# Block-sparse attention with a gated two-layer block behind it, one core: another load order at the start, weights and layer two moved, output stores on another queue

## The chip, the cores and the metric

The kernel runs on one core of one Trainium2 chip. The metric is the device time of one execution in microseconds, the median of several. A core has five engines that each work through their own list of instructions in order: PE (TensorE), DVE (VectorE), ACT (ScalarE), POOL (GpSimd) and SP (SyncE, which here only issues DMAs and loads registers). ACT and POOL issue DMAs too. They wait for each other through semaphores.

## The reference

Inputs are q, k, v of shape 4 x 8 x 768 x 64 (batches, heads, rows, width), three sampled block numbers for each of 24 blocks of 32 rows, and the weights of the second layer: w_in 512 x 1024, w_out 1024 x 512, g_ln 1024. `window` is 1. The heads of layer one's result are put side by side to x, 3072 x 512.

```python
    scores = scale * np.matmul(q, k.transpose(0, 1, 3, 2))
...
    mask = np.abs(blk_i - blk_j) <= window
    mask = mask | (blk_i == 0) | (blk_j == 0) | (blk_i == n_blocks - 1) | (blk_j == n_blocks - 1)
    for qb in range(n_blocks):
        for kb in sampled_blocks[qb]:
            mask[qb * block:(qb + 1) * block, kb * block:(kb + 1) * block] = True
    scores = np.where(mask, scores, -1000000000.0)
...
    attn = np.exp(scores)
    attn = attn / (np.sum(attn, axis=-1, keepdims=True) + 1e-09)
    return np.matmul(attn, v).astype(np.float32)
...
    h = x @ w_in
    h_max = np.max(h, axis=-1, keepdims=True)
    e = np.exp(h - h_max)
    sm = e / (np.sum(e, axis=-1, keepdims=True) + 1e-09)
    solu = h * sm
    mu = np.mean(solu, axis=-1, keepdims=True)
    var = np.mean((solu - mu) ** 2, axis=-1, keepdims=True)
    ln = (solu - mu) / np.sqrt(var + 1e-06) * g_ln
    return (ln @ w_out).astype(np.float32)
```

## The kernel before

**Layer one.** The work of a batch is four pairs of heads (16 pairs in all). k and q come from DRAM as float32, two heads to a DMA of 384 KB (`load_kq`, L302), are cast to bf16 (`cast_kq`, L310) and turned by PE (`turn_kq`, L316) into `kT` and `qT`. v comes in six DMAs of 256 KB (`load_v`, L325), is cast into `vbuf` (`cast_v`, L331), and the whole of it is written back to DRAM as bf16 rows (`save_v`, L335), so that the sampled blocks can be gathered from there. For each of 22 blocks of queries, `gather_k` (L364) copies the sampled key blocks inside SBUF, on POOL, DVE or ACT, and `gather_v` (L383) fetches the sampled value rows: as one indirect DMA on POOL, or as three or four plain DMAs on SP or ACT, whose addresses are loaded into registers first. `glob_k` and `glob_v` copy the first and the last block. `score_static` (L412) makes the scores of the band and of the first and last blocks in three parts, `score_rand` (L456) those of the sampled blocks in two. ACT takes exponentials into `pst` and `prd`, DVE multiplies by the band mask (L450). `out_list` and `out_mms` multiply by v in a first part that needs no gathered values and a second part that does (L507), and `normalise` writes `xb`.

**Layer two.** Tiles of 128 rows go in eight groups of three. `moe_x` (L534) turns `xb` into `xT` by three DMA transposes on SP; there is one `xT` buffer. A group is 15 steps: eight of `moe_f` (L547: four matmuls into the PSUM tile `hps`, an exponential on ACT, a product on DVE into `soluT`), one of `moe_s` (L562: sums), and six of `moe_o` (L598: two for each of three tiles; ACT scales the PSUM tile `ops` into `ot`, L610). `hps`, `ops` and the turned k and q share two PSUM buffers, `p_h`. `ot` has two buffers. The store of an `ot` tile is put off (`put_out`, L616): SP issues it just ahead of the next tile's `ot`, or at the next group's first step.

**Order.** The lists of the engines are in the order of the program, written out by hand. A loop over slots `s` (L780) deals out the work: six slots to a pair, layer one's parts first, then one step of layer two from slot `MOE0 = 31` on (two in every fourth slot, and two in each slot once layer one is done), then the loads, casts, turns and gathers. For batch `nb`, `f = s - 24 (nb - 1)` says when its loads, casts and gathers are issued (L835 to L860). The last slot of a batch's layer one is `s = 28, 52, 76, 100`; there `put_rows` and `moe_x` follow.

**Start.** Before the loop (L680 to L766) SP and ACT issue loads of k and q of batch 0, then v. All use the pool `raw`, which has four buffers, so that a load waits until an earlier one has been cast. DVE makes the tables of addresses (L704 to L743), then clears buffers (L744 to L760), then casts v. The remaining q of batch 0 is loaded in slots 0 to 2, and batch 0's gathers are dealt out in slots 3 to 5. In slot 5 POOL issues the load of `w_in` (L825, with a cast to bf16) and ACT those of `g_ln` and of `w_out` (`load_w`, L640: one DMA of 2 MB into `w_f`, which takes one of the two buffers of the pool `vgp`, tag `vg`, that the gathered values use). DVE scales `w_out` in slots 8 to 15 (`scale_w`) and takes its mean off it in slots 18 to 25 (`centre_w`).

Of the kernel before, what the change touches and what calls it, by code (L numbers as in the profile page):

```python
# [201 lines left out]
def kernel(  # L202
# [11 lines left out]
    nc = tc.nc  # L214
# [87 lines left out]
    def load_kq(b, which, a, eng):  # L302

        rw = raw.tile([TQ, 2, NT, D], FP32, tag="raw", name=f"raw{which}{b}_{a}")
        eng.dma_start(
            out=rw.rearrange("p h i d -> p h (i d)"),
            in_=(k, q)[which][b, 2 * a : 2 * a + 2].rearrange("h (p i) d -> p h (i d)", i=NT))
        staged[which, b, a] = rw
# [16 lines left out]
    def load_v(b, c, eng):  # L325
        rw = raw.tile([TQ, HD], FP32, tag="raw", name=f"rawv{b}_{c}")
        eng.dma_start(out=rw.rearrange("p (h d) -> p h d", h=H),
                      in_=v[b, :, c * TQ : (c + 1) * TQ, :].rearrange("h p d -> p h d"))
        staged[2, b, c] = rw
# [18 lines left out]
    def glob_k(b):  # L348
        z = kgz[b % 2]
        src = kTs[b].rearrange("p a (n o) -> p a n o", o=BLK)  # L350
        for par in range(2):
            lo = par * 64
            nc.gpsimd.tensor_copy(
                out=z[lo : lo + 64, :, lo : lo + 64].rearrange("p a (n o) -> p a n o", o=BLK),
                in_=src[lo : lo + 64, :, 0 : NB : NB - 1, :])
# [191 lines left out]
    def moe_f(g, f):  # L547
        hps = p_h.tile([128, GN], FP32, tag="h")
        for c in range(KD):
            nc.tensor.matmul(hps, w_in_sb[:, c, f * 128 : (f + 1) * 128], xTs[g][:, c, :],  # L550
                             start=(c == 0), stop=(c == KD - 1))
        if f == 0:
            sums_of[g] = p_sum.tile([128, 512], FP32, tag="sums", name=f"sums{g}")
        else:
            moe_e(g, f - 1)
        eTs[g, f] = mo3.tile([128, GN], BF16, tag="eT", name=f"eT{g}_{f}")
        nc.scalar.activation(out=eTs[g, f], in_=hps, func=ACT.Exp, scale=1.0)  # L557
        nc.vector.tensor_tensor(out=soluT[:, f, :, 0:128],  # L558
                                in0=hps.rearrange("p (i x) -> p i x", i=GT),
                                in1=eTs[g, f].rearrange("p (i x) -> p i x", i=GT), op=ALU.mult)  # L560
# [37 lines left out]
    def moe_o(g, i, half):  # L598
# [6 lines left out]
        if half == 1:  # L605
            if i == 0:
                moe_r(g)
            put_out()
            ot = mo.tile([128, d_model], FP32, tag="ot")
            nc.scalar.activation(out=ot, in_=o_ps.pop(t), func=ACT.Copy,  # L610
                                 scale=rstds[g][:, i : i + 1])
            ots.append((t, ot))

    ots = []

    def put_out():  # L616
        while ots:
            t, ot = ots.pop()
            nc.sync.dma_start(out=out[t * 128 : (t + 1) * 128, :], in_=ot)
# [3 lines left out]
    def moe_step(n):  # L623
# [3 lines left out]
        if r == 0:  # L627
            put_out()
# [10 lines left out]

    def load_w():  # L640
        w_f.append(vgp.tile([128, KF, d_model], FP32, tag="vg", name="w_f"))
        nc.scalar.dma_start(out=w_f[0], in_=moe_w_out.rearrange("(c p) m -> p c m", p=128))

    w_f = []

    def scale_w(c):
        nc.vector.tensor_scalar(out=w_out_sb[:, c, :], in0=w_f[0][:, c, :],
                                scalar1=g_ln_sb[:, c : c + 1], scalar2=None, op0=ALU.mult)
# [32 lines left out]
    load_kq(0, 0, 0, nc.sync)  # L681
    load_kq(0, 1, 0, nc.scalar)
    load_kq(0, 0, 1, nc.sync)
    load_kq(0, 0, 2, nc.scalar)
    cast_kq(0, 0, 0, nc.gpsimd.tensor_copy)
    cast_kq(0, 1, 0, nc.scalar.copy)
    load_kq(0, 0, 3, nc.sync)
    load_v(0, 0, nc.scalar)
    turn_kq(0, 0, 0, nc.scalar.copy)
    turn_kq(0, 1, 0, nc.scalar.copy)  # L690
    for c in range(3):
        cast_kq(0, 0, c + 1, nc.gpsimd.tensor_copy)
        load_v(0, c + 1, nc.sync)
# [50 lines left out]
    for vb in vbuf:  # L744
        nc.vector.memset(vb[:, :, :, D:D1], 1.0)
    zero_v = prd_p.tile([TQ, 2 * n_ed * BLK], BF16, tag="prd1", name="zero_v")
    nc.vector.memset(zero_v, 0.0)
    for b in range(B):
        nc.sync.dma_start(out=v_scr[b][NB * BLK :, :], in_=zero_v[0:BLK, 0 : H * D1])


    band = setup.tile([TQ, NCH, TQ], BF16, name="band")
    nc.vector.memset(band, 1.0)
    for j, i0, i1 in ((0, 2, 4), (1, 3, 4), (2, 0, 1), (3, 0, 2)):
        nc.vector.memset(band[j * BLK : (j + 1) * BLK, :, i0 * BLK : i1 * BLK], 0.0)
    nc.vector.memset(band[0:BLK, 0, :], 0.0)
    nc.vector.memset(band[TQ - BLK :, NCH - 1, :], 0.0)
    for z in kgz:
        nc.vector.memset(z, 0.0)
    nc.vector.memset(soluT[:, :, :, 128:D2], 1.0)  # L760
    for c in range(2):
        cast_v(0, c, nc.vector.tensor_copy)
        load_v(0, c + 4, nc.sync)
    for c in range(2, NCH):
        cast_v(0, c, (nc.vector.tensor_copy, nc.gpsimd.tensor_copy)[c % 2])
    save_v(0, 0, NCH, nc.sync)  # L766
    nc.vector.memset(mean_w, 1.0 / d_ff)
# [7 lines left out]
    MOE0 = 31  # L775
# [4 lines left out]
    while step < N_STEPS:  # L780
# [28 lines left out]
        if s < 3:  # L809
            load_kq(0, 1, s + 1, nc.sync)  # L810
        if 1 <= s < 4:
            turn_kq(0, 0, s, nc.scalar.copy)
        if s == 3:
            glob_k(0)
            glob_v(0, nc.gpsimd.tensor_copy)
        if 3 <= s < 6:
            cast_kq(0, 1, s - 2, nc.vector.tensor_copy)
            turn_kq(0, 1, s - 2, nc.vector.tensor_copy)
        if 3 <= s < 6:
            for i in range((s - 3) * 8, min((s - 2) * 8, n_gk)):  # L820
                gather_k(0, i, on=(1, 0, 1, 2)[i % 4])
                gather_v(0, i, on=(0, 1, 0, 1, 2)[i % 5])

        if s == 5:
            nc.gpsimd.dma_start(out=w_in_sb, in_=moe_w_in.rearrange("(c p) f -> p c f", p=128))  # L825
            nc.scalar.dma_start(out=g_ln_sb, in_=moe_g_ln.rearrange("(c p) -> p c", p=128))
            load_w()
        if 8 <= s < 8 + KF:
            scale_w(s - 8)
        if s == 17:  # L830
            mean_of_w()
        if 18 <= s < 18 + KF:
            centre_w(s - 18)

        for nb in range(1, B):  # L835
# [3 lines left out]
            for i in range(6):  # L839
                if f == 8 + i // 2:  # L840
                    load_v(nb, i, nc.sync)
                if f == 11 + i // 2:
                    cast_v(nb, i, (nc.vector.tensor_copy, nc.gpsimd.tensor_copy)[i % 2])
            for i in range(8):
                if f == 10 + i:
                    load_kq(nb, i // 4, i % 4, nc.sync)
                if f == 13 + i:
                    cast_kq(nb, i // 4, i % 4, nc.gpsimd.tensor_copy)
                if f == 15 + i:
                    turn_kq(nb, i // 4, i % 4, (nc.scalar.copy, nc.vector.tensor_copy)[i // 4])  # L850
            if f == 14:
                save_v(nb, 0, NCH, nc.sync)
                glob_v(nb, nc.gpsimd.tensor_copy)
            if f == 20:
                glob_k(nb)
            for i in range(n_gk):
                if f == 20 + i // 2:
                    gather_k(nb, i, on=(1, 2, 1, 2, 1, 0)[i % 6])
                if f == 17 + i * 14 // 22:
# [8 lines left out]
    put_out()  # L868
# [47 lines left out]
```

## Time and profile before

| | |
|---|---|
| median of three runs | 331.54 us (331.35 to 334.30) |
| profiled execution | 334.87 us, of which the span (first to last instruction) is 333.3 us |
| PE busy | 227.6 us, 68% of the span |
| DVE, ACT, POOL busy | 154.9, 155.0, 103.3 us |
| moved by DMA | 45.63 MB, 137 GB/s over the span |
| queue of SP (q1) | 34.81 MB; queue of ACT (q10) 3.62 MB; POOL's (q0) 6.58 MB |
| mean granted clock of PE | 0.903 |

How to read it: busy time of an engine leaves out register, branch and DMA-issuing instructions. The page cuts the span into 40 slices and gives for each the busy share in tenths (a digit for each), the clock granted to PE in tenths of full speed, and what the DMA engines did. In the timeline a row is: start, duration, engine and line, operation, output and inputs, shape, number of instructions in it, and in brackets the engine's idle time just before with what released it. SPq and ACTq are DMA-issuing instructions on those engines. The list of waits gives, for each pair of waiting engine and releaser, the total, the number of times and the longest.

### The profile page before, as it was taken

Reading aid. Unit: us, or ns where it says so; the run is one execution under the profiler, and the core shown is the slowest. Engines: PE = TensorE matmul, PEld = TensorE weight load, DVE = VectorE, ACT = ScalarE, POOL = GpSimd, SP = SyncE. Lnnn points to the kernel's source line nnn. Section 1 sums busy time; section 2 is a strip of 40 time slices with the busy share of each in tenths; the row PEclk is TensorE's granted clock in tenths of the full one; section 3 lists DMA queues with packets and bytes.
Section 4 is the critical chain, followed back from the end, with each engine's and each line's share of the span. In section 5 each row is a group of like instructions: output and inputs, shape, how many; then the busy total and the mean of one; then the engine's idle time right before and its main releaser. Section 6 shows DMA issues by size and latency. Waiting matters only on the chain.

```text
span 333.3 us, 9115 instructions
## 1 busy us (share of the span) xinstructions
PE 227.6 (68%) x3449; PEld 149.0 (45%) x3466; DVE 154.9 (46%) x490; ACT 155.0 (47%) x305; POOL 103.3 (31%) x170
## 2 busy tenths in 40 slices
PE   0502240679665899298918994989289999878991
PEld 0401230456543576166605663666156667335450
DVE  2833720464983364068803560598134535425340
ACT  2602230347673357077715662777256565233530
POOL 1335840136883106458500163585000000000000
PEclk9999999999955599879986999699759999959998
DMA  5748589879346759933358498432510410132202
GB/s 169 205 128 244 137 238 238 164 236 307 89 111 129 166 138 185 324 106 95 92 118 177 133 224 285 136 102 82 127 50 2 81 67 2 31 112 47 94 28 76
DMA packets 65233, 45.63 MB, mean 137 GB/s; under 512 B 43104, under 2 KB 59040, under 8 KB 65184
## 3 DMA queue, kind: packets, MB, share of 16 engines
q1 hardware_dynamic: 58016, 34.81, 40.2%
q0 software_dynamic: 2832, 6.58, 8.0%
q10 hardware_dynamic: 4336, 3.62, 3.7%
q8 instruction: 28, 0.46, 0.6%
q14 instruction: 21, 0.17, 0.2%
HBM read 33.26 MB, written 9.62 MB: 129 GB/s over the span
## 4 chain that ended last, share of the span: by engine, by line
PE 42%; DMA 24%; SPq 9%; DVE 8%; issue 6%; ACT 5%; POOL 2%; ACTq 1%; DVEq 0%; POOLq 0%
PE hps L550 12%; PE ops L603 10%; PE op L507 9%; DMA out_dram<-ot 7%; DMA raw<-in_k_dram 4%; DMA w_f<-in_moe_w_out_dram 4%; SPq L538 4%; PE sums L568 4%; SPq L394 3%; DMA vg<-v_scr 3%; DVE soluT L558 3%; PE ps L466 3%; PE ps L435 2%; ACT eT L557 2%; DVE xb L519 2%
## 5 line engine op out<-in xcount | busy, mean ns | idle before, releaser
L558 DVE TENSOR_TENSOR soluT<-hps,eT 128x384 bf16<-128x384 f32 x64 | 35.6, 558 | 102.3 <-ACT eT L557 102.1
L550 PE MATMUL hps<-xT,w_in_sb 128*128 128x384 bf16 x256 | 60.8, 369 | 18.7 <-ACT ot L610 11.6
L439 ACT ACTIVATE pst<-ps 128x1024 bf16<-128x1024 f32 x48 | 49.1, 1024 | 33.6 <-PE ps L435 31.8
L401 POOL DMA_INDIRECT vg<-v_scr,idx x48 | 47.8, 996 | 19.5 <-issue 12.9
L557 ACT ACTIVATE eT<-hps 128x384 bf16<-128x384 f32 x64 | 31.4, 490 | 41.5 <-PE hps L550 40.9
L320 PE MATMUL tp<-ident,st 128*128 128x128 bf16 x192 | 20.0, 256 | 37.9 <-DVE st L313 22.5
L603 PE MATMUL ops<-w_out_sb,soluT 128*128 128x512 bf16 x176 | 43.0, 380 | 1.1 <-issue 0.5
L550 PEld LDWEIGHTS <-w_in_sb 128*128 128x128 bf16 x256 | 23.3, 104 | 34.7 <-issue 22.4
L610 ACT ACTIVATE ot<-ops,rstd 128x512 f32<-128x512 f32 x24 | 16.5, 687 | 43.3 <-DMA out_dram<-ot 32.5
L507 PEld LDWEIGHTS <-pst 64*128 64x128 bf16 (+3 forms) x608 | 30.5, 110 | 12.4 <-DVE xb L519 6.2
L313 POOL CAST st<-raw 128x768 bf16<-128x768 f32 x28 | 23.4, 840 | 38.2 <-DMA raw<-in_k_dram 21.3
L320 PEld LDWEIGHTS <-st 128*128 128x128 bf16 x192 | 15.0, 114 | 42.9 <-DVE st L313 23.2
L470 ACT ACTIVATE prd<-ps 96x768 bf16<-96x768 f32 (+1 forms) x32 | 24.1, 756 | 10.1 <-PE ps L466 5.2
L332 POOL CAST v<-rawv 128x512 bf16<-128x512 f32 x11 | 7.0, 640 | 66.8 <-DMA rawv<-in_v_dram 49.2
L507 PE MATMUL op<-vg,prd 96*32 96x65 bf16 (+1 forms) x704 | 15.9, 212 | 14.0 <-DMA vg<-v_scr 14.0
L603 PEld LDWEIGHTS <-soluT 128*128 128x128 bf16 x192 | 17.0, 98 | 17.0
L507 PE MATMUL op<-v,pst 128*64 128x65 bf16 (+1 forms) x384 | 24.1, 211 | 0.0
L518 DVE RECIPROCAL recip_all<-op 128x7 f32<-128x7 f32 x32 | 6.4, 201 | 33.7 <-PE op L507 33.7
L466 PE MATMUL ps<-qT,kge 64*128 64x32 bf16 x320 | 8.5, 177 | 19.7 <-ACT kge L381 14.9
L507 PE MATMUL op<-vgl,pst 64*128 64x65 bf16 (+1 forms) x224 | 17.4, 207 | 5.4 <-DVE xb L519 5.3
L519 DVE TENSOR_TENSOR xb<-op,recip_all 128x448 bf16<-128x448 f32 x32 | 20.0, 625 | 1.2
L435 PE MATMUL ps<-qT,kT 64*128 64x128 bf16 (+1 forms) x384 | 19.8, 234 | 0.0
(100 smaller groups left out, 299.3 us busy)
## 6 DMA issues: line engine op xcount, KB each, us to landing
out_dram<-ot SPq DMA_DIRECT2D x24, 256.0 KB
rawv<-in_v_dram SPq DMA_DIRECT2D x23, 256.0 KB
raw<-in_k_dram SPq DMA_DIRECT2D x15, 384.0 KB
raw<-in_q_dram SPq DMA_DIRECT2D x15, 384.0 KB
vg<-v_scr SPq DMA_DIRECT2D x124, 32.5 KB
v_scr<-v SPq DMA_DIRECT2D x4, 780.0 KB
w_f<-in_moe_w_out_dram ACTq DMA_DIRECT2D x1, 2048.0 KB
w_in_sb<-in_moe_w_in_dram POOLq DMA_DIRECT2D x1, 1024.0 KB
```

Source lines behind the costliest of these rows:

```text
L313: copy(out=st.rearrange("p i h d -> p h i d"), in_=rw)
L320: nc.tensor.matmul(tp[:, i, :], st[:, i, :], ident, is_transpose=True, start=(i == 0), stop=(i == NT - 1))
L401: nc.gpsimd.indirect_dma_start(out=vgs[b][0:m, i, :], out_offset=None, in_=v_scr[b], in_offset=bass.IndirectOffsetOnAxis(ap=idx[0:m, qb : ...
L435: nc.tensor.matmul(ps[:, par, col : col + w], kT[:, c * TQ : (c + 1) * TQ], rhs, start=first, stop=(n == len(todo) - 1), skip_group_check= ...
L439: nc.scalar.activation(out=psts[pair][:, u], in_=ps, func=ACT.Exp, scale=scale)
L470: nc.scalar.activation(out=prds[pair, u], in_=ps[0:m, :, 0 : len(qbs) * BLK], func=ACT.Exp, scale=scale)
L507: nc.tensor.matmul(o, w, m, start=(i == 0), stop=(i == len(lst) - 1), skip_group_check=True)
L519: nc.vector.tensor_tensor(out=xbs[b][:, :, h * D : (h + 1) * D], in0=op[:, :, 0:D], in1=recip.broadcast_to([TQ, NSL, D]), op=ALU.mult)
L550: nc.tensor.matmul(hps, w_in_sb[:, c, f * 128 : (f + 1) * 128], xTs[g][:, c, :], start=(c == 0), stop=(c == KD - 1))
L557: nc.scalar.activation(out=eTs[g, f], in_=hps, func=ACT.Exp, scale=1.0)
L558: nc.vector.tensor_tensor(out=soluT[:, f, :, 0:128], in0=hps.rearrange("p (i x) -> p i x", i=GT), in1=eTs[g, f].rearrange("p (i x) -> p i ...
L603: nc.tensor.matmul(o_ps[t], soluT[:, f, i, 0:128], w_out_sb[:, f, :], start=(f == 0), stop=(f == KF - 1))
```

## The change

First batch: a tile `raw_v` for all of v and a tile `raw_kq` for seven of the eight k and q pieces take the two buffers of the pool `vgp` (tag `vg`) that are idle at the start; v is loaded first, by SP and ACT in turn, then k by SP and q by ACT, all of it before anything else. DVE clears its buffers before it makes the tables. v is cast by POOL and ACT, k and q by DVE; `glob_k` and `glob_v` of batch 0 move to DVE and slot 1, its gathers to slots 2 to 5 with the key copies on DVE and ACT only. Weights: `g_ln` and `w_out` are issued by SP in slot 9 (before, ACT in slot 5), `w_out` as two DMAs of 1 MB into buffers of the pools `kgi` and `kge`; its scaling and centring move to slots 14 to 21 and 24 to 31. `w_in` stays. Layer two starts at slot 33. For batches 1 to 3 the loads of v come three slots earlier, those of k and q and most else two; all of v is cast by POOL. The store of `ot` is issued by ACT right after `ot` is written. In the last two groups every second `hps` takes a buffer of the PSUM pool of the scores.

The diff, cut to its core:

```diff
-    def load_kq(b, which, a, eng):
+    def load_kq(b, which, a, eng, rw=None):
...
+        if rw is None:
+            rw = raw.tile([TQ, 2, NT, D], FP32, tag="raw", name=f"raw{which}{b}_{a}")
...
-    def load_v(b, c, eng):
+    def load_v(b, c, eng, rw=None):
...
-        hps = p_h.tile([128, GN], FP32, tag="h")
+        if g >= NG - 2 and f % 2:
+            hps = p_s.tile([128, 2, 512], FP32, tag="s", name=f"hs{g}_{f}")[:, 0, 0:GN]
+        else:
+            hps = p_h.tile([128, GN], FP32, tag="h", name=f"hps{g}_{f}")
...
-            put_out()
             ot = mo.tile([128, d_model], FP32, tag="ot")
             nc.scalar.activation(out=ot, in_=o_ps.pop(t), func=ACT.Copy,
                                  scale=rstds[g][:, i : i + 1])
-            ots.append((t, ot))
...
+            nc.scalar.dma_start(out=out[t * 128 : (t + 1) * 128, :], in_=ot)
...
+    w_f = [pl.tile([128, KF // 2, d_model], FP32, tag=tag, name=f"w_f{i}")
+           for i, (pl, tag) in enumerate(((kgi_p, "kgi"), (kge_p, "kge")))]
+
     def load_w():
-        w_f.append(vgp.tile([128, KF, d_model], FP32, tag="vg", name="w_f"))
-        nc.scalar.dma_start(out=w_f[0], in_=moe_w_out.rearrange("(c p) m -> p c m", p=128))
...
+        for i in range(2):
+            nc.sync.dma_start(
+                out=w_f[i],
+                in_=moe_w_out[i * d_ff // 2 : (i + 1) * d_ff // 2, :].rearrange(
+                    "(c p) m -> p c m", p=128))
...
-    load_kq(0, 0, 0, nc.sync)
-    load_kq(0, 1, 0, nc.scalar)
-    load_kq(0, 0, 1, nc.sync)
-    load_kq(0, 0, 2, nc.scalar)
-    cast_kq(0, 0, 0, nc.gpsimd.tensor_copy)
-    cast_kq(0, 1, 0, nc.scalar.copy)
-    load_kq(0, 0, 3, nc.sync)
-    load_v(0, 0, nc.scalar)
-    turn_kq(0, 0, 0, nc.scalar.copy)
-    turn_kq(0, 1, 0, nc.scalar.copy)
-    for c in range(3):
-        cast_kq(0, 0, c + 1, nc.gpsimd.tensor_copy)
-        load_v(0, c + 1, nc.sync)
+    raw_v = vgp.tile([TQ, NCH, HD], FP32, tag="vg", name="raw_v")
+    raw_kq = vgp.tile([TQ, 2 * NPR - 1, 2, NT, D], FP32, tag="vg", name="raw_kq")
+    for c in range(NCH):
+        load_v(0, c, (nc.sync, nc.scalar)[c % 2], raw_v[:, c, :])
+    for which in range(2):
+        for a in range(NPR):
+            i = which * NPR + a
+            load_kq(0, which, a, (nc.sync, nc.scalar)[which], raw_kq[:, i - 1] if i else None)
+    for vb in vbuf:
+        nc.vector.memset(vb[:, :, :, D:D1], 1.0)
...
+    for b in range(B):
+        nc.sync.dma_start(out=v_scr[b][NB * BLK :, :], in_=zero_v[0:BLK, 0 : H * D1])
...
-    for c in range(2):
-        cast_v(0, c, nc.vector.tensor_copy)
-        load_v(0, c + 4, nc.sync)
-    for c in range(2, NCH):
-        cast_v(0, c, (nc.vector.tensor_copy, nc.gpsimd.tensor_copy)[c % 2])
+    for c in range(NCH):
+        cast_v(0, c, (nc.gpsimd.tensor_copy, nc.scalar.copy)[c % 2])
     save_v(0, 0, NCH, nc.sync)
+    for which, a in ((0, 0), (1, 0)):
+        cast_kq(0, which, a, nc.vector.tensor_copy)
+        turn_kq(0, which, a, nc.scalar.copy)
...
-    MOE0 = 31
+    MOE0 = 33
...
-        if s < 3:
-            load_kq(0, 1, s + 1, nc.sync)
-        if 1 <= s < 4:
-            turn_kq(0, 0, s, nc.scalar.copy)
-        if s == 3:
-            glob_k(0)
-            glob_v(0, nc.gpsimd.tensor_copy)
-        if 3 <= s < 6:
-            cast_kq(0, 1, s - 2, nc.vector.tensor_copy)
-            turn_kq(0, 1, s - 2, nc.vector.tensor_copy)
-        if 3 <= s < 6:
-            for i in range((s - 3) * 8, min((s - 2) * 8, n_gk)):
-                gather_k(0, i, on=(1, 0, 1, 2)[i % 4])
+        for n in {0: (1, 2), 1: (3, 4), 3: (5,), 4: (6,)}.get(s, ()):
+            which, a = ((0, 1), (0, 2), (0, 3), (1, 1), (1, 2), (1, 3))[n - 1]
+            cast_kq(0, which, a, nc.vector.tensor_copy)
+            turn_kq(0, which, a, (nc.scalar.copy, nc.vector.tensor_copy)[which])
+        if s == 1:
+            glob_k(0, nc.vector.tensor_copy)
+            glob_v(0, nc.vector.tensor_copy)
+        if 2 <= s < 6:
+            for i in range((s - 2) * 6, min((s - 1) * 6, n_gk)):
+                gather_k(0, i, on=(1, 2)[i % 2])
                 gather_v(0, i, on=(0, 1, 0, 1, 2)[i % 5])
...
             nc.gpsimd.dma_start(out=w_in_sb, in_=moe_w_in.rearrange("(c p) f -> p c f", p=128))
-            nc.scalar.dma_start(out=g_ln_sb, in_=moe_g_ln.rearrange("(c p) -> p c", p=128))
+        if s == 9:
+            nc.sync.dma_start(out=g_ln_sb, in_=moe_g_ln.rearrange("(c p) -> p c", p=128))
             load_w()
-        if 8 <= s < 8 + KF:
-            scale_w(s - 8)
-        if s == 17:
+        if 14 <= s < 14 + KF:
+            scale_w(s - 14)
+        if s == 23:
             mean_of_w()
-        if 18 <= s < 18 + KF:
-            centre_w(s - 18)
+        if 24 <= s < 24 + KF:
+            centre_w(s - 24)
...
+                if f == 5 + i // 2:
+                    load_v(nb, i, nc.sync)
                 if f == 8 + i // 2:
-                    load_v(nb, i, nc.sync)
-                if f == 11 + i // 2:
-                    cast_v(nb, i, (nc.vector.tensor_copy, nc.gpsimd.tensor_copy)[i % 2])
+                    cast_v(nb, i, nc.gpsimd.tensor_copy)
             for i in range(8):
-                if f == 10 + i:
+                if f == 8 + i:
                     load_kq(nb, i // 4, i % 4, nc.sync)
+                if f == 11 + i:
+                    cast_kq(nb, i // 4, i % 4, nc.gpsimd.tensor_copy)
...
-            if f == 14:
+            if f == 12:
                 save_v(nb, 0, NCH, nc.sync)
...
-                if f == 20 + i // 2:
+                if f == 18 + i // 2:
                     gather_k(nb, i, on=(1, 2, 1, 2, 1, 0)[i % 6])
-                if f == 17 + i * 14 // 22:
+                if f == 15 + i * 15 // 22:
                     gather_v(nb, i, on=(0, 1, 0, 1, 0)[i % 5])
```

`put_out` and its calls are gone; DVE's memsets of `vbuf`, `zero_v`, `band`, `kgz` and `soluT` stand ahead of the tables. The turns of k and q of later batches go from `f == 15 + i` to `13 + i`, `glob_v` from 14 to 12 and `glob_k` from 20 to 18.

## The prediction

> **What bounds the kernel now.** I read the page's forty slices first (where PE is idle), then the list of waits (for whom), then the timeline around each hole.
>
> ```profile
> PE   0502240679665899298918994989289999878991
> PEclk9999999999955599879986999699759999959998
> DMA  5748589879346759933358498432510410132202
> GB/s 169 205 128 244 137 238 238 164 236 307 89 111 129 166 138 185 324 106 95 92 118 177 133 224 285 136 102 82 127 50 2 81 67 2 31 112 47 94 28 76
> ```
>
> One slice is 8.33 us. Where layer two runs, PE is at 8 or 9 tenths, so it is the bound there. The holes are the first six and a half slices, slice 7 (50 to 58 us, digit 0), and single slices later: the 17th (2), 21st (1), 25th (4) and 29th (2). At the 17th and 25th the DMA engines are at 9 or 8 tenths, at the 21st and 29th at about half: the same hole with two different neighbours. After each hole PEclk dips.
>
> ```profile
> ACT ot L610 <- DMA out_dram<-ot: 32.5, 5, 8.0
> PE op L507 <- DMA vg<-v_scr: 14.0, 4, 4.6
> PE hps L550 <- ACT ot L610: 11.6, 4, 6.3
> PEld L466 <- ACT kge L381: 15.1, 2, 8.1
> ```
>
> Columns: us in all, times, longest. ScalarE waited five times, 32.5 us, for an output store to land before it could write `ot` again (two buffers), and PE waited behind it: for the PSUM tile that ScalarE had not emptied, or for a key gather queued behind the stuck `ot` write.
>
> ```profile
> 60.79 0.21 PE L507 MATMUL op<-vg,prd 128*32 128x65 bf16 x1 [4.51 <-DMA vg<-v_scr]
> ...
> 127.62 0.69 ACT L610 ACTIVATE ot<-ops,rstd 128x512 f32<-128x512 f32 x1 [0.47 <-PE ops L603]
> ...
> 131.45 0.81 SPq L619 DMA_DIRECT2D out_dram<-ot  x1
> ...
> 141.73 1.44 PE L550 MATMUL hps<-xT,w_in_sb 128*128 128x384 bf16 x4 [6.27 <-ACT ot L610]
> ...
> 164.98 4.86 SPq L538 DMA_TRANSPOSE xT<-xb  x3
> ...
> 172.51 0.85 SPq L619 DMA_DIRECT2D out_dram<-ot  x2
> ...
> 176.27 0.21 PE L466 MATMUL ps<-qT,kge 64*128 64x32 bf16 x2 [7.97 <-ACT kge L381]
> ...
> 293.05 1.46 PE L550 MATMUL hps<-xT,w_in_sb 128*128 128x384 bf16 x4 [2.84 <-DMA xT<-xb]
> ```
>
> A bracket gives the idle time before an instruction and its releaser. See two things: the store of the tile written at 127.62 is issued only at 131.45, and in the other kind of hole it stands on SP behind three transposes and a gather (172.51). And four matmuls of `hps` take 1.44 us after a hole, 0.82 else (at 182.75, say). The same two holes come again before 208.73 (4.61 us) and 242.71 (6.94 us).
>
> **The change, part by part.** The sum is made against the profiled execution: 334.87 us, a span of 333.3 and 1.57 around it. The median of the runs is 331.54, 1% under it; the forecast is the gain taken off the median.
>
> **A. Start to the end of the first pair, -10.** All first-batch loads get a tile at once, v first. v is 1.57 MB; at the 169 to 205 GB/s of the first two slices it lands at 10 to 11 us, and three casts each on POOL (0.62) and ScalarE end by 13; the last v cast ended at 22.8 before. But the save of v stands on SP's queue behind four k loads, beside which ScalarE's four q loads run: 4.7 MB in all, at 205 to 244 GB/s done by 21 to 25. Its own landing took 5.02 us, some of it shared; I take 26, against 27.82. SP then issues nine gathers; six took from 27.84 to 41.57, 2.3 us each, so they end at 47 and land 2.4 to 3.5 later (38.95 2.43 and 27.84 3.52 in the chain). w_in still starts beside the last ones, w_f (14.49 us in the chain, with w_in beside it) no longer does: +1. So 51 instead of 60.8. Ends: -6 (SP stays the bound and w_in alone hurts as much as half of both), -15 (the save lands at 21). The batch-0 key copies leave POOL for DVE and ScalarE (eleven each, at 0.69 to 0.98 on ScalarE, less on DVE); both wait for gathers anyway. DVE's memsets (3.6 us, 13.66 to 17.25) move into its 5.23 us wait for the table's input: nothing, and 3.6 if the input came sooner. The moved `glob` copies (0.85 and 1.73 on POOL) and the k, q casts (0.56 on DVE) end before the save lands: nothing; at worst 2.6 later.
>
> **B. Weights on SP in slot 9, +5.** v of batch 1 now starts at about 47: 1.57 MB at 177 GB/s (slice 174.98 to 183.31) is 9 us, to 56. Then one k load, then w_f's 2.1 MB at 295 GB/s (130.9 to 140.9), 7 us, and behind it on SP the second k load: landed and cast (0.84) at 67. PE wants it in slot 14. Twenty slots took 38.0 us (60.9 to 98.9), 1.9 each, so slot 14 comes at 62. Five of the ten are given back. Ends 0 (transfers overlap better) and +9 (the q loads late too).
>
> **C. Layer two at slot 33, gathers and loads two or three slots earlier, -5.** Between 98.9 and 115.2 PE waits 1.85 us for `kge` copies (100.95), 1.60 for xT (105.32) and 1.77 for vg (109.56); all get two slots, about 4 us, of lead. Ends 0 and -8 (that stretch ran at clock 0.50). The two steps deferred run at the end, where the first `hps` of the seventh group waits 2.84 us for its transposes (287.97 to 293.05): 0, ends -1 and +2.
>
> **D. Stores on ScalarE's queue, -24.** PE idles 6.27 + 7.97 + 4.61 + 6.94 + 0.54 = 26.3 us. The first store now leaves at about 128.4 and its tile is wanted at 133.7, 5.3 us later; a lone store took 2.38 us to land, one behind 1.9 MB on SP's own queue 9.44. What is late next is xT: 5.1 us from 164.98 is 170.1, where PE, freed at 168.3, has 1.6 us of `op` first. I leave 2 us for stores landing late beside loads. Ends -13 (half) and -26. SP is rid of 24 issues (median 0.371, 9 us), which helps the gathers queued behind.
>
> From the DMA page of the Trainium skill (DMA: Bandwidth & Descriptors, Rules for kernel authors) comes a rule against this: spreading DMAs over SP, ACT and GpSimd brings no bandwidth, for all run on the same 16 engines; only issue time is saved. Were that all, the two holes with DMA at 0.91 (130.9 to 140.9, 199.5 to 208.8) would stay, and their 10.9 us with the clock's 3.6 be lost: 306. The rows with DMA at 0.48 (165.0 to 177.9, 232.4 to 244.3) speak of order, not bandwidth; for the other two the rule may hold in part.
>
> **E. Clock, -7.** After 141.73 matmuls run slow until 146.07: 4.3 us for what 2.5 would do (1.44 against 0.82). Four holes, 1.8 each. Ends -3, -9.
>
> **F. ScalarE's issues, +3.** 24 at 0.37 to 0.46 (ScalarE's load issues at 8.49 and 0.96), each behind its own 0.69 us write: 11 us. ScalarE is 56% busy from 115 to 288, but behind each stand exponentials that PE waits for, so a quarter counts. Ends 0 and +11. POOL takes nine more v casts (0.64 each, 5.8 us in three batches) from DVE; POOL is busy 26 of 49 us in 115.2 to 164.6: nothing, 5.8 without that cover.
>
> **G. Two more PSUM tiles in the last two groups, -3.** There a column block starts every 0.99 us (311.50, 312.50, 313.49), held by DVE (0.18 us each second time); with two blocks in hand, 115.76 and 116.50, 0.74. Sixteen at 0.2. Ends 0, -4.
>
> Sum: -10 + 5 - 5 + 0 - 24 - 7 + 3 - 3 = -41. 331.5 - 41 = 290.5, rounded 291.
>
> **Rivals.** *The stores still wait* (chance 0.16): for it, two gathers beside w_f and w_in, each on a queue of its own, landed 6 to 7 us after their issue ended (46.5 to 52.6, 48.9 to 56.0); against it, no such pair runs in layer two. D -13, E -3: -26, 306. *The start gives nothing* (0.15): the save behind the k loads, w_f before k of batch 1, and 0.50 clock staying; A -6, B +9, C 0 instead of -10: -28, 304. *All of it, and more* (0.10): A -15, B 0, C -8, the rest as taken: -54, 278. *Slower* (0.07): ScalarE becomes the bound by its issues. For it, three issues took 2.80 us at 38.57, and SP's stores up to 1.19; against it, SP's median is 0.37. It decides from 44 + the rest: without F the gain is 44, so each of the 24 must put 1.83 us on the path; at 2.2 us, 53 - 44 = +9, 340. That the stores are not issued from ScalarE's queue in fact has no support.
>
> **How the numbers follow.** The forecast, with its own range of 282 to 301, has 0.50. The two middle rivals at once, near 321, have 0.02. For 8 in 10 I take 278 to 310: it holds the forecast, both middle rivals and the edge of the good case. A measurement of this kernel can tell about 1% (328.2 to 334.9) from no change. Faster is the sum of the others, 0.93, less 0.03 for ScalarE near its deciding point: 0.90; within 1% 0.03; slower 0.07.
>
> **What would show it.** Right: no wait of ScalarE on out_dram above 2 us; no slice of 0 to 4 tenths for PE after 110; first pair ended at 46 to 54; a PE wait for k of batch 1 near 62 to 67; first `hps` with no xT wait; blocks of the last groups below 0.9 us. Wrong: ScalarE idle at its own issues with PE waiting for `eT` or `pst`; the save of v landing after 30; the clock at 0.5 where there is no hole.

## The result, and the profile after

The changed kernel takes 296.8 us (median of four runs, 295.18 to 299.75), the kernel before beside it 331.94: a ratio of 0.891 with a 95% interval of 0.885 to 0.898. The ratio leaves out one slow execution (299.75 us), so it says 36 us less where the two medians say 35; the text below goes by the ratio. In a second comparison, on another chip, it was 0.893 (0.884 to 0.902). The forecast was 291.

The profiled execution is that longest one, with a span of 298.2 us; the profile of the second comparison (299.5 of 297.83 to 300.35) has the same holes, each within 0.6 us of its length, and up to 2.1 us later.

The page's slices, now 7.46 us each:

```profile
PE   0044300779596499999985999999599999999990
...
PEclk9999999999869559999996899999979999999998
DMA  5984698999343599766459997552510220133211
```

PE works from the third slice on. Slices 6 and 7 (37 to 52 us, both 0) stand where the old hole at 50 to 58 us was: earlier, and longer. After 110 us only two slices are below 6, the 22nd (5) and the 29th (5), apart from the last. PEclk still dips, to 5 in slices 14 and 15 and to 6 in 12 and 22: holes of another kind are left.

The list of waits (us in all, times, longest):

```profile
PE ps L468 <- ACT kge L383: 15.2, 5, 10.4
PE op L509 <- DMA vg<-v_scr: 11.0, 3, 4.1
...
ACT ot L614 <- DMA out_dram<-ot: 1.4, 1, 1.4
```

ScalarE's wait for stores is gone, 1.4 us for 32.5. In its place stands PE waiting three times for a gather of v (`vg`). PE's waits for `kge` are as long in all as before (15.2 us, before 14.9), but they are others: the two behind a stuck `ot` (at 176.27 and 242.71 in the kernel before) are gone, and all of the 15.2 now lie at the start, where PE before waited for `vg` instead. The timeline around these:

```profile
37.09 0.83 POOL L817 DMA_DIRECT2D w_in_sb<-in_moe_w_in_dram  x1
39.52 6.31 ACTq L396 DMA_DIRECT2D vg<-v_scr  x3
42.19 4.26 SPq L396 DMA_DIRECT2D vg<-v_scr  x3
47.48 0.69 ACT L379 COPY kge<-kT 128x128 bf16 x3 [9.72 <-DMA vg<-v_scr]
...
48.43 0.24 PE L468 MATMUL ps<-qT,kge 64*128 64x32 bf16 x4 [10.37 <-ACT kge L383]
...
67.75 0.82 PE L321 MATMUL tp<-ident,st 128*128 128x128 bf16 x6 [2.68 <-POOL st L314]
...
95.22 3.95 SPq L540 DMA_TRANSPOSE xT<-xb  x3
99.94 1.33 SPq L396 DMA_DIRECT2D vg<-v_scr  x3
101.32 0.41 SPq L400 DMA_DIRECT2D vg<-v_scr  x1
103.21 0.21 PE L509 MATMUL op<-vg,prd 128*32 128x65 bf16 x1 [4.01 <-DMA vg<-v_scr]
...
159.92 0.21 PE L509 MATMUL op<-vg,prd 128*32 128x65 bf16 x1 [4.07 <-DMA vg<-v_scr]
...
216.08 0.19 PE L509 MATMUL op<-vg,prd 128*32 128x65 bf16 x1 [2.88 <-DMA vg<-v_scr]
```

Two things. From 39.52 the three DMAs of one gather are spread over 6.31 us of ScalarE's list, beside the load of `w_in`. Each of the three issues takes 0.32 us, so it is the time between them that is long. The key copies that stand behind them begin at 47.48, and PE waits 10.37 us for these. And from 95.22 SP issues three transposes, then, at 99.94, the last gather of the next batch's values: PE waits 4.01 us for it, and so again in the two batches that follow.

Where the time went is best read by stretches, from the first transposes of one batch to those of the next. The windows of the kernel before and of the changed one (start:end, length, then PE's busy time; PEclk and the share of the DMA engines near the end):

```profile
99.00:165.00 66.00, 52.21 (x826) 34.64 (x824) 33.80 (x105) 35.95 (x74) 30.90 (x47) 0.83 0.66 156
165.00:232.50 67.50, 52.88 (x861) 35.22 (x865) 33.20 (x104) 38.17 (x79) 26.48 (x40) 0.90 0.60 157
232.50:288.00 55.50, 47.20 (x788) 30.40 (x790) 23.45 (x70) 28.81 (x52) 0.00 (x0) 0.91 0.20 49
288.00:333.30 45.30, 31.96 (x219) 17.31 (x218) 14.36 (x42) 13.97 (x28) 0.00 (x0) 0.89 0.24 72
```

```profile
95.20:149.70 54.50, 46.73 (x807) 32.24 (x804) 32.30 (x97) 35.72 (x75) 28.76 (x44) 0.87 0.71 184
149.70:207.00 57.30, 51.22 (x862) 33.97 (x865) 32.42 (x101) 38.34 (x79) 27.70 (x43) 0.94 0.73 184
207.00:257.40 50.40, 46.15 (x786) 29.82 (x789) 22.40 (x62) 27.63 (x45) 0.00 (x0) 0.97 0.19 52
257.40:298.20 40.80, 31.08 (x232) 16.19 (x232) 15.78 (x50) 15.15 (x31) 0.00 (x0) 0.97 0.26 79
```

The start gives 3.8 us, the stretches 11.5, 10.2, 5.1 and 4.5. In the first three PE's idle time (length less busy) falls from 13.8 + 14.6 + 8.3 = 36.7 to 7.8 + 6.1 + 4.3 = 18.1 us, its busy time by 8.2: part of that is the clock, part that layer two is two steps further behind until the last stretch, which holds them.

### The profile page after: what moved, and what is told of

Its sections match the earlier page's. It is cut to its first block, busy times and chain, and to the rows that moved or that the text cites. A ratio compares the mean times of both kernels' runs of the same rounds, so it can differ in the third digit from the quotient of the medians.

```text
span 298.2 us, 9136 instructions
## 1 busy us (share of the span) xinstructions
PE 219.0 (73%) x3452; PEld 143.8 (48%) x3466; DVE 151.9 (51%) x488; ACT 160.6 (54%) x328; POOL 96.8 (32%) x149
## 4 chain that ended last, share of the span: by engine, by line
PE 45%; DMA 19%; SPq 11%; DVE 9%; ACT 6%; issue 5%; ACTq 1%; POOL 1%; DVEq 0%; POOLq 0%
PE hps L555 11%; PE ops L608 10%; PE op L509 9%; SPq L396 5%; DMA vg<-v_scr 5%; SPq L540 4%; DMA raw<-in_k_dram 3%; DMA raw_kq<-in_k_dram 3%; DMA raw_v<-in_v_dram 3%; PE sums L573 3%; DMA rawv<-in_v_dram 3%; DVE xb L521 3%; ACT eT L562 2%; PE ps L468 2%; DVE soluT L563 2%
## 5 line engine op out<-in xcount | busy, mean ns | idle before, releaser
L441 ACT ACTIVATE pst<-ps 128x1024 bf16<-128x1024 f32 x48 | 49.0, 1023 | 17.7 <-PE ps L437 13.4
L563 DVE TENSOR_TENSOR soluT<-hps,eT 128x384 bf16<-128x384 f32 x56 | 31.3, 559 | 51.1 <-ACT eT L562 51.0
L403 POOL DMA_INDIRECT vg<-v_scr,idx x48 | 46.7, 974 | 24.8 <-ACT pst L441 12.1
L555 PE MATMUL hps<-xT,w_in_sb 128*128 128x384 bf16 x224 | 46.7, 336 | 1.0 <-issue 0.7
L608 PE MATMUL ops<-w_out_sb,soluT 128*128 128x512 bf16 x179 | 45.6, 398 | 2.0 <-issue 0.8
L562 ACT ACTIVATE eT<-hps 128x384 bf16<-128x384 f32 x56 | 27.4, 489 | 20.5 <-PE hps L555 19.5
L321 PEld LDWEIGHTS <-st 128*128 128x128 bf16 x192 | 14.6, 114 | 34.2 <-DVE st L314 26.9
L608 PEld LDWEIGHTS <-soluT 128*128 128x128 bf16 x192 | 17.8, 101 | 19.5 <-issue 3.2
L555 PEld LDWEIGHTS <-w_in_sb 128*128 128x128 bf16 x256 | 20.8, 98 | 12.7 <-issue 2.4
L314 POOL CAST st<-raw 128x768 bf16<-128x768 f32 x24 | 19.9, 831 | 20.3 <-DMA raw<-in_k_dram 12.5
L334 POOL CAST v<-rawv 128x512 bf16<-128x512 f32 x18 | 11.6, 645 | 44.0 <-DMA rawv<-in_v_dram 43.7
L468 PE MATMUL ps<-qT,kge 64*128 64x32 bf16 x320 | 7.9, 176 | 17.7 <-ACT kge L383 15.2
L324 ACT COPY kT<-tp 128x768 bf16<-128x768 bf16 x16 | 12.8, 801 | 14.8 <-PE tp L321 14.8
## 6 DMA issues: line engine op xcount, KB each, us to landing
vg<-v_scr SPq DMA_DIRECT2D x124, 32.5 KB
```

What stands on the lines that cost most here:

```text
L314: copy(out=st.rearrange("p i h d -> p h i d"), in_=rw)
L321: nc.tensor.matmul(tp[:, i, :], st[:, i, :], ident, is_transpose=True, start=(i == 0), stop=(i == NT - 1))
L403: nc.gpsimd.indirect_dma_start(out=vgs[b][0:m, i, :], out_offset=None, in_=v_scr[b], in_offset=bass.IndirectOffsetOnAxis(ap=idx[0:m, qb : ...
L441: nc.scalar.activation(out=psts[pair][:, u], in_=ps, func=ACT.Exp, scale=scale)
L563: nc.vector.tensor_tensor(out=soluT[:, f, :, 0:128], in0=hps.rearrange("p (i x) -> p i x", i=GT), in1=eTs[g, f].rearrange("p (i x) -> p i ...
L608: nc.tensor.matmul(o_ps[t], soluT[:, f, i, 0:128], w_out_sb[:, f, :], start=(f == 0), stop=(f == KF - 1))
```

## The experiments

Two theories of the main gain stood against each other. **Theory 1**, as forecast: it comes from the stores leaving SP's queue. **The rival**: it comes from the next batch's loads and layer two's steps being shifted against each other, which takes the stores out from behind the loads by itself. Kernels of one comparison ran on one chip; their times are given as ratios to the kernel before on that chip, and us are the ratio times its median there.

**Stores alone.** The kernel before, with only this edit:

```diff
-            put_out()
...
-            ots.append((t, ot))
+            nc.scalar.dma_start(out=out[t * 128 : (t + 1) * 128, :], in_=ot)
```

> The kernel before with one part of the change alone: each output store is issued by ScalarE right after its tile is written. Theory 1 (the stores waited for their turn in SP's order and in its queue): the five waits of PE, 26.3 us, go, but each batch boundary shows what stood behind them, the transposes and the last value gather on SP, so 14 to 22 us are gained: 310 to 318 us, and no wait of ScalarE for a store above 2 us. Theory 2 (the stores waited for DMA bandwidth): the two holes beside the loads of k and q stay, 8 to 13 us are gained at most: 319 to 324 us, with ScalarE still waiting 4 to 8 us for a store near 140 and 208 us.

Measured: 0.964 (0.953 to 0.974), 12 us of 336. That is under the 14 to 22 of theory 1, although the waits that this edit was to remove are gone:

```profile
PE op L507 <- DMA vg<-v_scr: 18.3, 6, 6.6
PE ps L466 <- ACT kge L381: 7.2, 4, 3.6
PE hps L550 <- DMA xT<-xb: 5.7, 2, 4.1
...
ACT ot L609 <- DMA out_dram<-ot: 2.8, 2, 2.1
```

ScalarE's waits for stores are 2.8 us, and where PE stood 6.27 and 7.97 us in the kernel before (141.73, 176.27) its longest gaps are 2.95 and 3.56, for a cast by POOL and a key copy by ScalarE. But the first stretch (102.5 to 166.8 us in this kernel) is still 64.3 us long, for 66.0, with PE busy 53.43 instead of 52.21. So 26.3 us of idle time that ended at stores were not 26.3 us to gain: other waits took part of the place. The stores' queue alone is worth a third of the change.

**All but the stores.** The changed kernel with the stores put off and issued by SP, as before.

```diff
+            put_out()
             ot = mo.tile([128, d_model], FP32, tag="ot")
...
-            nc.scalar.dma_start(out=out[t * 128 : (t + 1) * 128, :], in_=ot)
+            ots.append((t, ot))
```

> The changed kernel with the stores put off and issued by SP again, as before; all else as changed. Theory 1: ScalarE waits for stores again at each batch boundary, where three transposes stand ahead of them on SP: 10 to 20 us slower than the changed kernel, 307 to 317 us. Rival (the loads two to three slots earlier and layer two two slots later would have taken the stores out of the way by themselves): 0 to 4 us slower, 297 to 301 us.

Measured: 0.899 (0.890 to 0.907), against 0.891 and 0.893 for the whole change (measured on other chips): some 2 us, and the intervals overlap. The profile shows why:

```profile
ACT ot L615 <- DMA out_dram<-ot: 14.3, 3, 9.7
...
PE hps L555 <- ACT ot L615: 4.2, 2, 3.2
```

ScalarE still waits three times for a store, 14.3 us, but only 4.2 us of it reaches PE, in two waits. So the stores' queue is worth 12 us if it is changed first and some 2, perhaps nothing, if it is changed last. Theory 1 falls; what is left of the change gives 34 us by itself.

**Loads early alone, and layer two late alone.** Two kernels, each the kernel before with one edit.

```diff
-                if f == 8 + i // 2:
+                if f == 5 + i // 2:
                     load_v(nb, i, nc.sync)
...
-                if f == 10 + i:
+                if f == 8 + i:
                     load_kq(nb, i // 4, i % 4, nc.sync)
...
-                if f == 17 + i * 14 // 22:
+                if f == 15 + i * 15 // 22:
                     gather_v(nb, i, on=(0, 1, 0, 1, 0)[i % 5])
```

(with the casts, turns, the save of v and the key gathers two or three slots earlier in the same way, and with all of v cast by POOL, as in the changed kernel), and

```diff
-    MOE0 = 31
+    MOE0 = 33
```

> The kernel before with only the loads, casts, turns and gathers of batches 1 to 3 placed as in the changed kernel (k, q two slots, v three slots earlier); the stores stay on SP, layer two stays at slot 31. Theory 1, the stores waited because the next batch's 1.9 MB stood ahead of them, and it is the earlier loads that took most of this away: ScalarE's waits for out_dram fall from 32 us to 10 to 18 us and the time by 10 to 18 us, ratio 0.945 to 0.97. Rival, layer two's later slot did it: the waits stay above 25 us, ratio 0.985 to 1.01.

> The kernel before with only layer two started at slot 33 instead of 31. Theory 1 (the earlier loads took the stores' waits away): only the two waits for xT go (4.4 us), ratio 0.98 to 0.995, ScalarE's waits for out_dram stay above 25 us. Rival (the later slot moves the stores off the loads): the waits fall to 10 to 18 us, ratio 0.945 to 0.97.

Measured: loads early 0.947 (0.938 to 0.955), 18 us; layer two late 0.988 (0.979 to 0.998), 4 us. The early loads are the largest single piece of the change. The shift and the v casts that go from DVE to POOL were not run apart; but in the kernel before DVE casts only nine pieces of v in batches 1 to 3, some 0.4 us each, and waits for none of them, so the shift is the likelier part. In that kernel the stores still go through SP; its wait for stores, its timeline, and windows from 102 us on:

```profile
ACT ot L610 <- DMA out_dram<-ot: 17.7, 4, 5.2
```

```profile
129.05 1.04 SPq L305 DMA_DIRECT2D raw<-in_q_dram  x2
130.95 1.89 SPq L394 DMA_DIRECT2D vg<-v_scr  x3
132.94 0.37 SPq L619 DMA_DIRECT2D out_dram<-ot  x1
...
159.37 4.21 SPq L538 DMA_TRANSPOSE xT<-xb  x3
163.68 0.53 SPq L619 DMA_DIRECT2D out_dram<-ot  x1
```

```profile
102.00:159.40 57.40, 50.67 (x815) 33.66 (x816) 32.67 (x101) 35.91 (x72) 30.52 (x46) 0.86 0.72 177
159.40:218.50 59.10, 53.63 (x866) 35.14 (x864) 33.40 (x101) 37.77 (x79) 28.09 (x43) 0.91 0.74 179
218.50:269.70 51.20, 47.49 (x792) 30.41 (x791) 22.59 (x62) 27.66 (x48) 0.00 (x0) 0.93 0.25 51
```

The store that stood among the q loads at 131.45 is now issued when the last of them is out (132.94 after 129.05), and the one that stood behind transposes and gathers at 172.51 follows the transposes at once (163.68). ScalarE's waits fall from 32.5 to 17.7 us, none above 5.2, and PE's idle time in the three stretches from 36.7 to 6.7 + 5.5 + 3.7 = 15.9 us, less than in the changed kernel (18.1).

With layer two late, ScalarE's waits for stores fall even further, to 10.2 us, as the rival said; but the time barely moves, as theory 1 said for that kernel. Neither theory had both. Its wait for stores, and its windows:

```profile
ACT ot L610 <- DMA out_dram<-ot: 10.2, 3, 4.8
```

```profile
101.85:163.91 62.06, 50.26 (x811) 34.22 (x812) 31.98 (x96) 35.24 (x70) 30.10 (x47) 0.81 0.66 166
163.91:229.29 65.38, 57.70 (x866) 36.86 (x865) 33.49 (x104) 38.30 (x78) 25.92 (x40) 0.84 0.69 161
229.29:282.00 52.71, 49.23 (x790) 30.74 (x789) 23.48 (x70) 28.55 (x51) 0.00 (x0) 0.90 0.19 52
```

PE's idle time in these is 23.0 us, 13.7 less than before, while its busy time is 157.2, 4.9 more, at a clock of 0.81, 0.84 and 0.90 (0.83, 0.90, 0.91 before). Fewer us of ScalarE waiting for stores is no measure of the gain. Why the clock was lower there stays open.

**The last gather first.** The new wait of PE for `vg` is put down to the last gather of v standing on SP behind the transposes. The changed kernel with the 22 gathers dealt over 13 slots instead of 15, so that the last goes out before the transposes:

```diff
-                if f == 15 + i * 15 // 22:
+                if f == 15 + i * 13 // 22:
```

> The changed kernel with the value gathers of batches 1 to 3 spread over 13 slots instead of 15, so that the last of them is issued two slots earlier, ahead of the three transposes. Theory 1 (what took the place of the store waits is the last gather, behind the transposes on SP: PE waits 4.01, 4.07 and 2.88 us at 103, 160 and 216 us): these go, and 5 to 10 us with them: 287 to 292 us. Rival (xT or the third output tile is late right behind it): 0 to 3 us, 294 to 297 us, with an equal wait for xT or the output tile near the same places.

Measured: 0.871 (0.862 to 0.879), 7 us better than the whole change's 0.891 and 0.893 (on other chips), with intervals that do not overlap.

```profile
93.18 0.41 SPq L400 DMA_DIRECT2D vg<-v_scr  x1
96.49 3.93 SPq L540 DMA_TRANSPOSE xT<-xb  x3
```

The last gather is out at 93.18, ahead of the transposes, as in the two batches that follow, and no wait of PE for `vg` is left in the list. That cause is shown. xT, which the forecast named as the next thing to be late, does not appear either.

**w_in away from the gathers.** The changed kernel with POOL's load of `w_in` in slot 20 instead of 5:

```diff
-        if s == 5:
+        if s == 20:
             nc.gpsimd.dma_start(out=w_in_sb, in_=moe_w_in.rearrange("(c p) f -> p c f", p=128))
```

> The changed kernel with the load of w_in in slot 20 instead of slot 5. Theory 1 (w_in beside the last gathers starves them, and ScalarE, which issues some of them, stands still, so that PE waits 10.4 us near 48 us): most of that wait goes, and as less is queued ahead of the second batch's loads little is given back: 5 to 10 us faster than the changed kernel, 287 to 292 us. Rival (SP's own issue of nine gathers, ended at 47 us, bounds the start): at most 2 us, 295 to 298 us, with the wait moved from the key copies to the gathered values.

Measured: 0.878 (0.868 to 0.889), 4 to 5 us better than the whole change; this interval overlaps that of the change at its edge, and the gain is at or just under the low end of the 5 to 10 us expected. The rows that answer to 39.52, 42.19 and 47.48:

```profile
39.78 2.37 ACTq L396 DMA_DIRECT2D vg<-v_scr  x3
42.40 1.55 SPq L396 DMA_DIRECT2D vg<-v_scr  x3
43.64 0.69 ACT L379 COPY kge<-kT 128x128 bf16 x3 [5.70 <-DMA vg<-v_scr]
```

The three DMAs of one gather are out of ScalarE within 2.37 us instead of 6.31, those of another out of SP within 1.55 instead of 4.26, and the copies behind start 3.8 us earlier. The stretch of one row is not the measure that repeats: in the kernel with the last gather first, which also loads `w_in` in slot 5, ScalarE's three lie within 2.88 us, but begin only at 43.70. What repeats is when the copies behind begin: between 47.31 and 48.64 in four profiled executions with `w_in` in slot 5, at 43.64 here and at 43.55 in another with it in slot 20 (on the slowest chip 51.51 to 52.91 against 50.34). A wait of 5.70 is left, since ScalarE still stands at gathers before its key copies.

**Both.** The last two edits together, on two chips; the second time beside the changed kernel itself.

> The changed kernel with both edits: w_in in slot 20, and the value gathers of later batches over 13 slots. If the two waits lie in different places and nothing else stands right behind them, the gains add: 10 to 19 us faster than the changed kernel, 278 to 287 us. Rival (one store of work stands behind both, such as the DMA of the second batch or PE's slow clock): no more than the larger of the two, 287 to 292 us.

> The changed kernel itself, as the control of the runs beside it: ratio to the kernel before 0.88 to 0.90, as in the first comparison (0.891). In the profile the three waits of PE for the last value gather behind SP's transposes (2.9 to 4.1 us each) and the wait of PE for ScalarE's kge of about 10 us near 48 us come again if they belong to the program; if they were of that one execution, they are gone.

> The changed kernel with w_in loaded in slot 20 and the value gathers two slots shorter, beside the control this time. If the two waits are independent, the gains add: about 4 us for w_in (first half of the first pair 4 to 6 us earlier) and about 7 us for the gathers, ratio 0.85 to 0.87. Rival: the two share one cover, since a batch that starts earlier also asks for its gathers earlier, and the sum is no more than the gathers alone, 0.87 to 0.88.

Measured: on the first chip 0.885 (0.870 to 0.900). There every kernel was slower, the kernel before 354.9 us, and the changed kernel itself was not run beside it, so this one is read only against the others of that chip (0.925 to 0.946). On the second, 0.893 (0.884 to 0.902) for the change and 0.860 (0.852 to 0.868) for both: 287.36 us against 299.03 and 335.52. The single gains, 0.020 to 0.023 and 0.013 to 0.015, add up to 0.033 to 0.038; 0.033 was measured. Within these intervals the two gains add, and this is the fastest version.

**Three single parts** of the change undone, beside each other on that slower chip: layer two back at slot 31; the two extra PSUM tiles taken out; and k and q loaded ahead of v.

```diff
-    MOE0 = 33
+    MOE0 = 31
```

```diff
-        if g >= NG - 2 and f % 2:
-            hps = p_s.tile([128, 2, 512], FP32, tag="s", name=f"hs{g}_{f}")[:, 0, 0:GN]
-        else:
-            hps = p_h.tile([128, GN], FP32, tag="h", name=f"hps{g}_{f}")
+        hps = p_h.tile([128, GN], FP32, tag="h", name=f"hps{g}_{f}")
```

```diff
-    for c in range(NCH):
-        load_v(0, c, (nc.sync, nc.scalar)[c % 2], raw_v[:, c, :])
     for which in range(2):
         for a in range(NPR):
...
+    for c in range(NCH):
+        load_v(0, c, (nc.sync, nc.scalar)[c % 2], raw_v[:, c, :])
```

> The changed kernel with layer two starting at slot 31, as before, instead of 33. Theory 1 (the two slots are lead for the transposes of each batch boundary, and the two steps put off fill the last wait for xT): 3 to 8 us slower than the changed kernel, 300 to 305 us, with waits of PE for xT at the boundaries and 3 us before the seventh group. Rival (the last gather is late there anyway, so the lead is not used): within 2 us, 295 to 299 us.

> The changed kernel without the two more PSUM tiles in the last two groups. Theory 1: blocks come every 0.99 us again instead of 0.74; 16 of them, 4 us slower: 299 to 302 us. Rival (ScalarE and DVE hold the same pace anyway, or the end is bound by the stores): 0 to 1 us.

> The changed kernel with the first batch's k and q loaded ahead of v, into the same tiles. Theory 1 (the save of v and the gathers behind it set the start; k and q have slack): the save lands later by what k and q's 3.1 MB took, less what stood in the queue ahead of it anyway, 0 to 4 us later: 296 to 301 us. Rival A (v first is what the start gains by): 8 to 12 us slower, 305 to 309 us. Rival B (k and q are late in the changed kernel, PE being idle until 17 us): 2 to 4 us faster.

Measured: 0.946 (0.938 to 0.954), 0.925 (0.917 to 0.933) and 0.927 (0.909 to 0.945). The kernel without the PSUM tiles is the same as the change up to the seventh group, so until then it stands in for the control.

The tiles are read from the blocks, not from the totals. From the last `ot` of one group to the last of the next takes 15.3 us without them and 13.8 with them, in the seventh group as in the eighth (288 to 303 and to 318; with them, in the kernel with k and q first, 294 to 308 and to 322): 1.5 us each, 3.0 in all, where 4 was expected. The seventh group without them:

```profile
290.12 0.81 PE L552 MATMUL hps<-xT,w_in_sb 128*128 128x384 bf16 x4 [0.36 <-DVE soluT L560]
290.84 0.81 PE L552 MATMUL hps<-xT,w_in_sb 128*128 128x384 bf16 x4
292.10 0.81 PE L552 MATMUL hps<-xT,w_in_sb 128*128 128x384 bf16 x4 [0.36 <-DVE soluT L560]
```

Every second block waits for DVE: 1.98 us for two blocks, 0.99 each, as in the kernel before. With them a block starts every 0.74 us.

With layer two at slot 31 the span is 330.7 us; without the tiles it is 325.9, and would be 322.9 with them, so that slot 31 costs 7.8 us by these two executions, 1.2 of which stand ahead of the first transposes (108.15 for 106.99), before the slot can matter. By the medians of all runs (334.4, and 327.4 less 3.0) it is 10 us; 3 to 8 was expected. Its list has PE waiting for xT:

```profile
PE hps L555 <- DMA xT<-xb: 10.6, 4, 4.2
```

So xT is what is late next only as long as layer two starts at slot 31; with the loads early and slot 31 in the kernel before there were the same four waits, 10.6 us. The later slot is worth some 7 to 10 us where the loads are early, and 4 where they are not.

With k and q first, SP's gathers begin at 26.61 instead of 24.71, and the first transposes at 109.22 instead of 106.99: v first is worth about 2 us at the end of the first batch, within the 0 to 4 of theory 1; over the whole kernel the intervals are too wide to tell.

## Why the prediction was right or wrong

The time, the sign and the holes' places came out; the forecast of -41 against -36 measured is near because two terms that were wrong in opposite ways belong to the same idle time; that the two errors nearly cancelled was luck. By its own steps:

**A, start, -10: mis-sized.** The save of v had landed by 24.69 (26 taken), SP's nine gathers ended at 47.34 (47 taken). But the +1 for `w_in` beside the last gathers failed: beside `w_in` the three DMAs of one gather were spread over 6.31 us of ScalarE's list, and the key copies behind them held PE 10.4 us. The reciprocal at the end of the pair's first half came at 56.50 for 61.04, 4.5 us earlier instead of 10. With `w_in` moved away it came at 53.81, 7.2 us earlier, and the whole kernel gained 4 to 5 us; the 2.8 us still missing were not traced.

**B, weights on SP, +5: right in place, half in size.** PE waits for k at 67.75, where 67 was forecast, for 2.68 us. A and B together: -4.0 us at the first transposes (95.22 for 99.20), -5 forecast; -4.5 and +2.7 leave 2 us that were gained elsewhere in the first batch and not traced.

**C, -5, and D, -24: the attribution failed.** The step that failed is D's first sentence, which took 26.3 us of PE's idle time because a wait for `out_dram` ended it. That the stores stood behind the next batch's loads was right, and read from the rows (131.45, 172.51). It was not seen that C, in the same change, moves those loads away by two or three slots and so removes the same holes: C was priced only by the three small waits after 98.9 us. Alone, the loads' shift (with the v casts on POOL) is worth 18 us, layer two's slot 4, the stores' queue 12; the last, on top of the rest, some 2. C, D, E and F were forecast at -33; the whole change less the start's 4 and G's 3 is -29, and that still holds the three waits for the late gather, which cost 7 us.

These three waits are the second failed step of D: "What is late next is xT". It was the last gather of v, on SP behind the very transposes that xT waits for. The rows for it were there: 109.56, PE waiting 1.77 us for `vg`, and in the kernel before SP issuing gathers after the transposes of 99.20. It was counted in C as a wait that two slots of lead would end.

The Trainium skill's page DMA: Bandwidth & Descriptors (Issuing engines are not separate DMA queues) says that DMAs of all issuing engines run on the same 16 DMA engines, and that another issuing engine saves only issue time. For the whole change that came nearer than the forecast: moving the stores last was worth some 2 us. Alone it was worth 12. The 24 issues take SP some 9 us in all, but what the rows show there is order: at 131.45 and 172.51 a store stands in SP's list behind loads and transposes, and the first takes 9.44 us more to land. The same page (Queues, rings and completion order) says that each DMA engine takes a ring's descriptors in order and goes round between the queues, and that would fit both numbers: a store on another queue passes the loads ahead, and gains little where none are ahead. No run here shows the rounds themselves.

**E, clock, -7: open.** PE's busy time fell by 8.2 us in the first three stretches, which is of that size, but a part of it is the two deferred steps, and dips are left behind the new waits. In the run with layer two late alone the clock was lower in all three stretches although the holes shrank, so the reckoning by four holes of 1.8 us is not shown.

**F, ScalarE's issues, +3: not contradicted, not isolated.** A store's issue takes ScalarE 0.34 to 0.39 us, and the gap from `ot` to its next work, which holds the issue, is mostly 0.41 to 0.47. The list has 6.7 us of such gaps; PE's waits for ScalarE there are some tenths each. No kernel was run with the stores on a third queue.

**G, -3: right.** 3.0 us by the blocks, with the place and the step (0.99 to 0.74) as read.

Of the rivals, "the stores still wait" fell on its place (1.4 us of waits); "the start gives nothing" was nearer on A (-6 taken, -4.5 measured) but not on B (+9 taken, +2.7 measured).

## What to carry to other kernels

Before a wait is priced, ask of every other part of the change whether it removes the same wait; two parts that open one hole are worth the hole once, and running each part alone on the kernel before and all but it on the kernel after shows this. On a queue that works in order, look at what stands ahead of each late transfer (here a store behind loads, then a gather behind transposes): moving the one ahead by two or three slots can bring as much as moving the late one to another queue. After a long wait is removed, list everything that the same queue issues in that place, and not only the next reader.

## What the runs showed of the hardware

Beside the load of `w_in` on POOL's queue, small DMAs on two other engines' queues were issued later: the key copies behind ScalarE's began at 47.31 to 48.64 us with it and at 43.55 and 43.64 without (on the slowest chip 51.51 to 52.91 and 50.34). A single issue took ScalarE 0.32 us either way; the time between the issues grew. The DMA engines were 0.90 busy there with `w_in` (37.1 to 47.0) and 0.47 without (37.1 to 44.0). That it is a load with a cast was not shown to matter.

The same kernel differs between chips by more than most parts of this change: the kernel before took 331.9, 335.5, 336.0 and 354.9 us (medians). On the slowest chip SP issued its first eighteen DMAs that gather v over 17.96 us, on another over 11.68, with the same instructions. What is behind that was not settled.

The mean granted clock of an execution does not order the times: two executions of the changed kernel on one chip had 0.868 and 0.945 and took 299.5 and 300.35 us, two on another 0.855 and 0.949 and took 296.35 and 297.25.
